# Attention and a routed MLP on one core: router rows on 128 partitions, gathered rows scaled by ScalarE and added by TensorE, late statistics moved, dummy products in the head, and a new order

## The chip, the core and the metric

The kernel runs on one NeuronCore of a Trainium2 chip. The core has five engines with instruction queues of their own: TensorE (PE, with PEld for its weight loads), VectorE (DVE), ScalarE (ACT), GpSimd (POOL) and SyncE (SP, here a queue of DMAs). They meet at semaphores; each runs its own queue strictly in order. The metric is the device time of one execution, in microseconds, as the median of several runs.

## The reference

Two blocks in a row on x of 2048 rows (tokens) and 448 columns, with layer norms ahead of both. The first is attention with 16 heads of 28 columns that share one key and one value head. The second scores each row with one vector, takes the best 8 rows of all 2048, and runs those 8 alone through a gated MLP of 1792 columns; the other rows pass unchanged.

```python
def _A_ref(x, wq, wk, wv, wo):
    q = (x @ wq).reshape(B, S, H, Dh).transpose(0, 2, 1, 3)
    k = x @ wk
    v = x @ wv
    p = _softmax(jnp.einsum("bhqd,bkd->bhqk", q, k) * (Dh ** -0.5), axis=-1)
    o = jnp.einsum("bhqk,bkd->bhqd", p, v)
    return o.transpose(0, 2, 1, 3).reshape(B, S, H * Dh) @ wo
def _B_ref(x, w_r, w_gate, w_up, w_down):
    r = x @ w_r
    idx = jnp.argsort(-r, axis=-1)[:, :8]
    x_sel = x[idx]
    y = (_silu(x_sel @ w_gate) * (x_sel @ w_up)) @ w_down
    y = y * _sigmoid(r[idx])
    return x + scatter(y, idx)
h = x + _A_ref(_layernorm(x), ...)
h2 = h + _B_ref(_layernorm(h), ...)
```

(shortened; the second block's residual is the normed h, so the output is h plus its norm, and for 8 rows the MLP's y on top)

## The kernel before

**Tiles.** The rows are cut into 16 blocks of 128 queries (b) and 16 tiles of 128 keys (j). A pair (b, j) has the scores of 16 heads: four strips of 128 x 512 in PSUM, made by matmuls on 32-row pieces of K (`scores`, L823). Their exponentials are made by one of two engines. On ScalarE (`act_tile`, `spill`) one ACTIVATE covers two strips, 128 x 1024, and writes P (L888). On VectorE with POOL (`dve_tile`) one TENSOR_SCALAR covers one strip and writes Y, a 16-bit integer whose bits are a rough exponential (L915); POOL adds a constant to a whole tile twice (Yc, L926), and the three versions, with values of their own weight, sum to a better one. So an ACT tile costs ScalarE two instructions and PE one group of value products; a DVE tile costs VectorE four, POOL two and PE three groups. `_ND` says how many tiles of each block go to VectorE: 87 of 256 in all. Six ACTIVATEs of block 1 run early and write into the still empty MLP weights (wg_sb, wu_sb, L874); `_EARLY` says behind how many tiles of block 0.

**Head.** `group(g)` norms a few key tiles: statistics on VectorE (bn, mv, L724), the scale on ScalarE (var, rstd), scaled rows in `of`, transposes on PE (L757) with a copy to xnT (L762), then K, V and for each block Q (`q_project`). K has two halves of partitions that hold the same keys. VectorE copies both from PSUM (L772, r = 0 and 1), or, for the groups in `_KD`, only the first, and two DMAs copy it on. POOL makes the masks tri and ident and clears K and Vs.

**Block's end.** `evict` copies the sums (Ot, L953), sends the denominators through DRAM, inverts them (Rc) and fetches them broadcast (Rb); VectorE multiplies (On, L966); `out_proj` projects, adds x, takes statistics and the router's dot product (junk, L1001), and `ln2` writes the output rows. Rows also go to `n_rows` in DRAM for a later gather.

**Tail.** `stage1` finds the best 8 of each of the first 14 blocks (best, idx), DMAs their numbers (gidx, cidx), gathers these 112 rows, and norms them again (cst, xc). `tail` finishes block 15 through PSUM alone. `last_rows` takes its statistics. A row of 112 + 256 scores on one partition (uc) is searched for its maximum 8 (top8, idx8); a product with ones sends the positions to all partitions (q16, one16), a comparison makes a one-hot matrix (oh), and products with it pick the 8 rows (xsel) and their numbers (tok). Then come gate, up and down products. The 8 output rows are read back by an indirect DMA (base, once all output rows are written), VectorE adds the MLP's yT to them (fin), and an indirect DMA writes them. `warm` runs products that nobody reads, so that PE doesn't stand idle.

**Order.** Nothing of the order on an engine is written by hand. `_Flow.plan` is a list scheduler in the kernel: each operation has a duration that the author gives, reads, writes, and a priority; the plan picks the next one for each engine, and assigns PSUM banks. The tables ahead of it (`_W`, `_LOOK`, `_WIN`, `_LATE`, `_HOLD`) steer it. So any change of a duration or a table can reorder all queues; semaphores keep the result right whatever the times. L628 is the helper that issues most matmuls, L640 that of the DMAs.

Of the kernel before, what the change touches and what calls it, by code (L numbers as in the profile page):

```python
# [25 lines left out]
class _Graph:  # L26
# [214 lines left out]
_KD = (1, 2, 4)  # L241
_EARLY = (0, 6, 9)
# [6 lines left out]
    0, 0, 0, 0, 0, 0, 0, 0, 0, 0, 0, 0, 0)  # L249
# [264 lines left out]
def _fast(nc, G, sb, ps, psb, flag, scr, rows, A_x, A_wq, A_wk, A_wv, A_wo, B_w_r, B_w_gate, B_w_up, B_w_down, out):  # L514
# [204 lines left out]
    def group(g):  # L719
# [29 lines left out]
        for a in range(t0, t1, 2):  # L749
# [9 lines left out]
            G.op(PE, [tr(k, ch) for k in range(m) for ch in range(NCH)], m * 4 * (150 if g == 0 else 80),  # L759
                 reads=[("of", a + k) for k in range(m)] + ["ident"], writes=[u.key], take=u)  # L760
# [8 lines left out]
                  for ch in range(NCH)], 4 * (145 if g == 0 else 5 + w / 2.4), reads=[("wkr", r) for r in range(4)] + ["wk_rep"] + [("xnT", t) for t in tl_],  # L769
# [47 lines left out]
    def scores(kind, b, j, k, key, tile=None, slot=(), parts=()):  # L817
# [15 lines left out]
        o = G.op(PE, [part(q, *p) for q, p in enumerate(parts)] if parts else strip, 231,  # L833
# [14 lines left out]
    def pv_op(b, key, src, v, j, reads):  # L848
# [7 lines left out]
        o = G.op(PE, [fn(i) for i in range(4)], 231, form="P", reads=reads + [("V", j), "Vone%d" % v], prio=key,  # L856
# [10 lines left out]
    def spill(end):  # L867
        while strips:
            if strips[0][0] == 1 and strips[0][1] in early:
                b, j, _, key = strips[0]  # L870
                for k, i in enumerate((0, 2)):
# [8 lines left out]
            if len(strips) < n or (end and len(strips) == 4 and n == 3):  # L880
                if not end:
# [7 lines left out]
                                                           scale=OCT), 50.0 + 426.5 * n,  # L889
# [977 lines left out]
```

## Time and profile before

| | |
|---|---|
| median of 3 runs | 348.11 us (347.79 to 348.26) |
| the profiled execution | 348.56 us, span 346.6 us |
| busy in the span | PE 318.2, ACT 325.4, DVE 319.4, POOL 190.8 us |
| ACTIVATE of scores (P) | 332, and 6 early ones |
| strips on VectorE (Y) | 348 |

A group's row has line, engine, operation, output <- input with shapes and count, then its busy time and the mean length of one in ns, then idle time of its engine just ahead of it and what ended it. A time line's row has start and length in us. The mean of an ACTIVATE is longer than its share of the time, since the next one begins before the last one's end is recorded; two starts give the pace.

### The profile page before, as it was taken

The page shows a single profiled execution, that of the slowest core. Times are in us where ns is not written, and L with a number is a line of the kernel's source. Part 1 is how long each engine was busy: PE and PEld are TensorE (multiplying, and loading weights), DVE is VectorE, ACT ScalarE, POOL GpSimd, SP SyncE. Part 2 cuts the span into 40 slices and gives each one's busy share as a digit, 9 for nine tenths or more (in the row PEclk, how much of TensorE's full clock was granted, in tenths as well). Part 3 has the DMA queues.
Part 4 walks back from the last instruction along what each step waited for, and adds up shares of the span by engine and source line. Part 5 has one row for each costly group of instructions (what it writes and reads, how often), then busy time and mean ns, then how long its engine had stood idle before and what let it go on. Part 6 is the DMA issues. An engine that isn't in the chain of part 4 may idle for free.

```text
span 346.6 us, 8725 instructions
## 1 busy us (share of the span) xinstructions
PE 318.2 (92%) x3630; PEld 105.2 (30%) x3630; DVE 319.4 (92%) x662; ACT 325.4 (94%) x387; POOL 190.8 (55%) x206
## 2 busy tenths in 40 slices
PE   3889899999999999999999998999999999999974
PEld 2644232323232322323232322323232322222334
DVE  6998997999988999999899899999999899999874
ACT  5599999999999999999999999999999999999850
POOL 8010475666545648667456566576747456775401
PEclk9999999999999999999999999999999999999995
DMA  6510000000020205020020206020101012152210
GB/s 158 138 40 3 0 3 18 20 17 18 5 85 4 84 4 168 27 60 30 8 80 5 84 4 165 4 46 16 33 4 30 7 58 85 42 152 58 60 36 9
DMA packets 18374, 16.18 MB, mean 47 GB/s; under 512 B 6574, under 2 KB 15438, under 8 KB 18330
## 3 DMA queue, kind: packets, MB, share of 16 engines
q1 hardware_dynamic: 16826, 15.01, 15.5%
q8 instruction: 29, 0.48, 0.6%
q10 hardware_dynamic: 1392, 0.45, 0.6%
q0 software_dynamic: 112, 0.12, 0.1%
q14 instruction: 15, 0.12, 0.1%
HBM read 11.78 MB, written 3.71 MB: 45 GB/s over the span
## 4 chain that ended last, share of the span: by engine, by line
ACT 83%; DVE 9%; DMA 3%; PE 3%; issue 0%; POOLq 0%; POOL 0%; ACTq 0%; DVEq 0%
ACT P L888 80%; DVE Y L915 4%; PE ps L628 2%; DMA wqx<-in_A_wq_dram 1%; ACT wg_sb L874 1%; DMA wqx<-n_rows,cidx 1%; DVE bn L724 1%; PE ps L823 1%; DMA cidx<-gidx 1%; ACT wu_sb L874 1%; DVE K L772 0%; ACT wqx L711 0%; DVE Q L806 0%; PE ps L757 0%; DVE gidx L1123 0%
## 5 line engine op out<-in xcount | busy, mean ns | idle before, releaser
L888 ACT ACTIVATE P<-ps 128x1024 bf16<-128x1024 f32 x332 | 306.8, 1287 | 0.0
L926 POOL INT64_ADD Yc<-Y x174 | 178.5, 1037 | 127.7 <-DVE Y L915 112.3
L915 DVE TENSOR_SCALAR Y<-ps 128x512 int16<-128x512 f32 x348 | 220.0, 683 | 12.0 <-PE ps L823 11.3
L823 PE MATMUL ps<-Q,K 32*128 32x512 bf16 (+1 forms) x1024 | 147.1, 386 | 14.1 <-ACT P L888 10.8
L823 PEld LDWEIGHTS ps<-Q,K 32*128 32x128 bf16 (+1 forms) x1024 | 37.7, 91 | 142.9 <-ACT P L888 122.1
L853 PE MATMUL ps<-Yc,Vs 128*32 128x512 bf16 x696 | 63.9, 385 | 0.0
L853 PE MATMUL ps<-P,Vs 128*32 128x512 bf16 x664 | 59.4, 387 | 0.0
L853 PE MATMUL ps<-Y,Vs 128*32 128x512 bf16 x348 | 34.2, 384 | 0.2 <-DVE Ot L953 0.2
L853 PEld LDWEIGHTS ps<-P,Vs 128*32 128x32 bf16 x664 | 14.1, 93 | 28.3 <-issue 26.2
L853 PEld LDWEIGHTS ps<-Yc,Vs 128*32 128x32 bf16 x696 | 15.7, 94 | 21.5 <-issue 15.8
L628 PE MATMUL ps<-xnT,wqx 112*128 112x128 bf16 x256 | 21.6, 229 | 0.0
L628 PE MATMUL ps<-wo_pad,On 128*32 128x448 bf16 (+1 forms) x244 | 18.1, 358 | 1.2 <-DVE Y L915 0.6
L628 PEld LDWEIGHTS ps<-xnT,wqx 112*128 112x128 bf16 x256 | 15.6, 102 | 7.7 <-issue 4.8
L806 DVE TENSOR_SCALAR Q<-ps,qone 128x512 bf16<-128x512 f32 (+1 forms) x16 | 11.6, 727 | 1.0 <-PE ps L628 0.9
L853 PEld LDWEIGHTS ps<-Y,Vs 128*32 128x32 bf16 x348 | 9.1, 94 | 9.3 <-issue 7.4
L966 DVE TENSOR_TENSOR On<-Ot,Rb 128x512 bf16<-128x512 f32 x15 | 11.0, 734 | 0.5 <-DMA Rb<-l_scr 0.5
L757 PE MATMUL ps<-ident,of 128*112 128x128 bf16 x64 | 6.3, 248 | 5.5 <-DVE of L737 5.5
L996 DVE TENSOR_TENSOR of<-ps,x_sb 128x448 bf16<-128x448 f32 x15 | 9.3, 619 | 1.1 <-PE ps L628 1.1
L953 DVE COPY Ot<-ps 128x512 f32<-128x512 f32 x15 | 10.3, 685 | 0.0
L724 DVE BATCH_NORM_STATS2 bn<-x_sb 128x6 f32<-128x448 bf16 x16 | 9.5, 610 | 0.0
L998 DVE BATCH_NORM_STATS2 bn<-of 128x6 f32<-128x448 bf16 x15 | 9.3, 622 | 0.1
L1001 DVE SCALAR_TENSOR_TENSOR junk<-of,w_rb 128x448 bf16<-128x448 bf16 x14 | 8.5, 611 | 0.0
(169 smaller groups left out, 141.4 us busy)
## 6 DMA issues: line engine op xcount, KB each, us to landing
Rb<-l_scr SPq DMA_DIRECT2D x15, 256.0 KB
out_dram<-of SPq DMA_DIRECT2D x16, 112.0 KB, 2.2
n_rows<-of SPq DMA_DIRECT2D x14, 113.0 KB, 2.4
x_sb<-in_A_x_dram SPq DMA_DIRECT2D x3, 448.0 KB, 4.4
wg_sb<-in_B_w_gate_dram SPq DMA_DIRECT2D x3, 448.0 KB, 6.1
wu_sb<-in_B_w_up_dram SPq DMA_DIRECT2D x3, 448.0 KB, 6.1
xnT<-in_B_w_down_dram SPq DMA_DIRECT2D x3, 448.0 KB, 7.7
wqx<-in_A_wq_dram ACTq DMA_DIRECT2D x1, 392.0 KB, 4.6
```

The source lines that it names most:

```text
L628: return lambda e: e.matmul(o() if callable(o) else o, lhsT=l, rhs=r, start=start, stop=stop)
L724: G.op(DV, lambda e, t=t: e.bn_stats(bn6[:, t, :], x_sb[:, t, :]), 516, reads=[("x", t)], writes=[("bn6", t)], after=[G.last_w[("xnT", 0)] ...
L806: G.op(DV, lambda e, c=c, src=src: e.tensor_scalar(Q[:, b % 3, c[0]:c[1], :], src(), qone[:, 0:1], None, ALU.add), 60 + n * 150, reads=[u. ...
L823: return e.matmul(ps[:, u.b[0] + q, :], lhsT=K[a:a + w, i % 2, j * 128:(j + 1) * 128], rhs=Q[a:a + w, b % 3, :, :].rearrange("p h n -> p ( ...
L853: return e.matmul(ps[32 * i:32 * i + 32, ACC, :], lhsT=Vs[:, v, j, :], rhs=src(i), start=info["first"] == o.idx, stop=info["last"] == o.idx)
L888: G.op(AC, lambda e, u=u, p=p, n=n: e.activation(P[:, p:p + n, :], ps[:, u.b[0]:u.b[0] + n, :], ACT.Exp, bias=EB, scale=OCT), 50.0 + 426.5 ...
L915: G.op(DV, lambda e, u=u, g0=g0: e.tensor_scalar(Y0[:, g0, :].bitcast(I16), ps[:, u.b[0], :], 0.0, TOP - STEP[-1], ALU.max, ALU.min), 599, ...
L926: G.op(PO, lambda e: e.int64_add(Yc[:, c, :, :].rearrange("p a b -> p (a b)").bitcast(I64), Y0[:, 4 * s:4 * s + 4, :].rearrange("p a b -> ...
L953: o = G.op(DV, lambda e: e.tensor_copy(Ot[:, rb, :], ps[:, ACC, :]), 598, reads=[pk(ACC)], writes=[("Ot", rb)], prio=b - 10.0, after=blk[b ...
L966: G.op(DV, lambda e: e.tensor_tensor(On[:, rb, :, :].rearrange("p h n -> p (h n)"), Ot[:, rb, :], Rb[:, rb, :], ALU.mult), 599, reads=[("O ...
L996: G.op(DV, lambda e: e.tensor_tensor(of[:, t, 0:D], hp(), x_sb[:, t, :], ALU.add), 535, reads=[u.key, ("x", t)], writes=[("of", t)], free=u)
L998: G.op(DV, lambda e: e.bn_stats(bn6[:, t, :], of[:, t, 0:D]), 520, reads=[("of", t)], writes=[("bn6", t)])
```

## The change

- **Tiles.** `_ND` sums to 90: three tiles go from ScalarE to VectorE and POOL. `_EARLY` puts the early ACTIVATEs behind three tiles of block 0. `_KD` is (3, 5): K of tiles 1, 2, 3, 6 and 7 gets its second half from VectorE, that of tiles 4, 5 and 8 to 11 by DMA.
- **Planner's numbers.** Durations, hops and tables are new, so all queues are ordered anew.
- **Head.** `fill` issues products of a constant tile into a bank that nobody reads: 44 at the start, 28 more between the first groups. Both halves of block 0's Q are copied by ScalarE. The masks wait for POOL's first 64-bit addition.
- **Block 14.** Its dot product with the router's vector no longer waits for its scale and is multiplied by it later; its statistics stand behind the shuffles of block 15, its scale behind their exponentials, and its output rows on ScalarE behind xc. So do those of block 15.
- **Router.** Scores are multiplied out to all 128 partitions (weights broadcast), so that maximum, positions and one-hot need no send. The 112 best are searched first and replaced by their 8 (a maximum that writes into PSUM), so the last maximum runs over 264 elements; the positions are still searched in 368.
- **Gathered rows.** xc is made by ScalarE (scale and bias) instead of VectorE.
- **End.** The base rows are added by PE (a product with the identity into the same bank), and the two halves of fin are copied by VectorE and ScalarE. The check of the denominators stands behind xsel.

```diff
-_KD = (1, 2, 4)
-_EARLY = (0, 6, 9)
+_KD = (3, 5)
+_EARLY = (3, 3, 3)
-_ND = (2, 7, 6, 3, 7, 7, 6, 5, 5, 7, 6, 5, 4, 5, 6, 6)
+_ND = (2, 6, 7, 4, 6, 6, 5, 7, 6, 6, 5, 6, 7, 5, 6, 6)
-_LOOK = 111.5
+_LOOK = 167.8
...
+    def fill(n, ns, after):
+        G.op(PE, [mm(ps[:, ACC, 0:128], idi[:, :], idi[:, :], True, True) for _ in range(n)], n * ns, reads=["idi"],
+             writes=[pk(ACC)], after=after, prio=-1999)
+
+    fill(44, 98, ())
...
     G.op(PO, lambda e: e.affine_select(ident[:, :], idi[:, :], [[-1, 128]], ALU.is_equal, 0.0, base=0, channel_multiplier=1),
-         300, reads=["idi"], writes=["ident"])
+         300, reads=["idi"], writes=["ident"], after=[lib])
...
         if g == 0:
+            fill(5, 56, [G.last_w[uk.key][0]])
             q_project(0)
+            fill(9, 56, [o for o in G.ops[-8:] if o.eng == PE][-1:])
...
-            if b == 0 and c[0] == 0:
+            if b == 0:
                 G.op(AC, lambda e, c=c, src=src: e.activation(Q[:, 0, c[0]:c[1], :], src(), ACT.Identity, bias=qone[:, 0:1]),
...
             G.op(AC, lambda e, u=u, p=p, n=n: e.activation(P[:, p:p + n, :], ps[:, u.b[0]:u.b[0] + n, :], ACT.Exp, bias=EB,
-                                                           scale=OCT), 50.0 + 426.5 * n,
+                                                           scale=OCT), 64.0 + 426.7 * n,
...
-        G.op(AC, lambda e: e.activation(st[:, t, 1:2], st[:, t, 0:1], ACT.Exp, scale=-0.5), 200, reads=[("st0", t)],
-             writes=[("st1", t)])
+        q = G.op(AC, lambda e: e.activation(st[:, t, 1:2], st[:, t, 0:1], ACT.Exp, scale=-0.5), 200, reads=[("st0", t)],
+                 writes=[("st1", t)])
+        for o in late15:
+            o.deps[q.idx] = False
+            o.deps[G.last_w["xc"][0].idx] = False
...
-        G.op(AC, lambda e: e.activation(of[:, t, 0:D], hp(), ACT.Identity, bias=st[:, t, 3:4], scale=st[:, t, 2:3]), 560,
+        o = G.op(AC, lambda e: e.activation(of[:, t, 0:D], hp(), ACT.Identity, bias=st[:, t, 3:4], scale=st[:, t, 2:3]), 560,
              reads=[u.key, ("st2", t), ("st3", t)], writes=[("of", t)], free=u)
+        o.deps[G.last_w["xc"][0].idx] = False
...
-        G.op(DV, lambda e: e.tensor_scalar(gidx[:, :], idx1[:, :], base1f[:, 0:1], None, ALU.add), 70,
-             reads=["idx1", "base1f"], writes=["gidx"])
+        G.op(DV, lambda e: e.tensor_scalar(gidx[:, :], idx1[:, :], base1f[:, 0:1], None, ALU.add), 100,
+             reads=["idx1", "base1f"], writes=["gidx"], lock=True)
...
-        G.op(DV, lambda e: e.tensor_scalar(xc, candb, cm[:, 0:1], cst[:, 4:5], ALU.subtract, ALU.mult), 400,
-             reads=["cand", "cst4"], writes=["xc", "wq_sb", "wq_pad"] + [("wqp", c) for c in range(NCH)], lock=True)
+        G.op(DV, lambda e: e.tensor_scalar(cst[:, 5:6], cm[:, 0:1], -1.0, cst[:, 4:5], ALU.mult, ALU.mult), 62,
+             reads=["cand", "cst4"], writes=["cst5"])
+        G.op(AC, lambda e: e.activation(xc, candb, ACT.Identity, bias=cst[:, 5:6], scale=cst[:, 4:5]), 560,
+             reads=["cand", "cst4", "cst5"], writes=["xc", "wq_sb", "wq_pad"] + [("wqp", c) for c in range(NCH)], prio=-60)
...
-        comb = bank(uc, slice(0, 1), slice(0, NB + 256))
-        G.op(DV, lambda e: e.max(top8[:, :], comb()), 510, reads=[uc.key], writes=["top8"], prio=-48.5)
...
-        G.op(DV, lambda e: e.tensor_copy(q16[:, :], idx8[:, :]), 62, reads=["idx8"], writes=["q16"], prio=-48.5)
-        G.op(PE, mm(bank(uo, c=slice(0, 8)), one16[:, :], q16[:, :], True, True), 100, reads=["one16", "q16"],
-             writes=[uo.key], take=uo)
+        G.op(DV, lambda e: e.max(bank(uc, c=slice(NB + 256, NB + 264))(), bank(uc, c=slice(0, NB))()), 250, reads=[uc.key],
+             writes=["uc2"])
+        G.op(DV, lambda e: e.max(top8[:, :], bank(uc, c=slice(NB, NB + 264))()), 450, reads=["uc0", "uc1", "uc2"],
+             writes=["top8"], prio=-48.5)
+        G.op(DV, lambda e: e.max_index(idx8[:, :], top8[:, :], bank(uc, c=slice(0, NB + 256))()), 570,
+             reads=[uc.key, "uc0", "uc1", "top8"], writes=["idx8"], prio=-48.5, free=uc)
...
+                fns += [mm(bank(uy[h], slice(0, 8), yc), ident[0:8, 0:8], base[:, dc], True, False),
+                        mm(bank(uy[h], slice(0, 8), yc), yT[:, c, :], ident[:, 64 * (c // 3):128], False, True)]
+        G.op(DV, lambda e: e.tensor_copy(fin[:, half[0]], ps[0:8, uy[0].b[0], 0:256]), 330, reads=[uy[0].key], writes=["fin0"],
+             free=uy[0])
+        G.op(AC, lambda e: e.activation(fin[:, half[1]], ps[0:8, uy[1].b[0], 0:192], ACT.Copy), 330, reads=[uy[1].key],
+             writes=["fin1"], free=uy[1])
```

Line numbers of the changed kernel differ by a few to twenty: P is L896, Y L923, On L974, gidx L1135, base L1277.

More of the change, by code (lines that the diff above doesn't have):

```diff
@@ L758, in tr @@
                                              of[:, a + k, ch * CK + cut(a, ch):(ch + 1) * CK + cut(a, ch)], ident[:, :])
-            G.op(PE, [tr(k, ch) for k in range(m) for ch in range(NCH)], m * 4 * (150 if g == 0 else 80),
-                 reads=[("of", a + k) for k in range(m)] + ["ident"], writes=[u.key], take=u)
+            o = G.op(PE, [tr(k, ch) for k in range(m) for ch in range(NCH)], m * 4 * (100 if g == 0 else 80),
+                     reads=[("of", a + k) for k in range(m)] + ["ident"], writes=[u.key], take=u)
+            if g == 0:
+                fill(8, 56, [o])
+            elif g == 1:
+                fill(6, 56, [o])
             dst = xnT[0:CK, :, a * 128:(a + m) * 128]
@@ L855, in fn @@
             return run
-        o = G.op(PE, [fn(i) for i in range(4)], 231, form="P", reads=reads + [("V", j), "Vone%d" % v], prio=key,
+        o = G.op(PE, [fn(i) for i in range(4)], 226, form="P", reads=reads + [("V", j), "Vone%d" % v], prio=key,
                  after=[blk[b - 1]["evict"] if b else None])
@@ L1011, in ln2 @@
         sv = of[:, sl, D:RW].bitcast(F32)
-        G.op(AC, lambda e: e.activation(st[:, sl, 0], sv[:, :, 1], ACT.Ln, bias=ebias[:, 0:1]), 300,
-             reads=[("stf", t) for t in ts] + ["ebias"], writes=[("st0", t) for t in ts])
-        G.op(AC, lambda e: e.activation(st[:, sl, 1], st[:, sl, 0], ACT.Exp, scale=-0.5), 100, reads=[("st0", t) for t in ts],
+        ln = G.op(AC, lambda e: e.activation(st[:, sl, 0], sv[:, :, 1], ACT.Ln, bias=ebias[:, 0:1]), 175,
+                  reads=[("stf", t) for t in ts] + ["ebias"], writes=[("st0", t) for t in ts])
+        G.op(AC, lambda e: e.activation(st[:, sl, 1], st[:, sl, 0], ACT.Exp, scale=-0.5), 87, reads=[("st0", t) for t in ts],
              writes=[("st1", t) for t in ts])
@@ L1229, in tail @@
                      reads=[(nm, c) for c in range(4)] + [nm + "0", "xsel"], writes=[uh[k].key], take=uh[k])
-        G.op(AC, lambda e: e.activation(sig[:, 0:8], ps[:, ut.b[0], 8:16], ACT.Exp, scale=-1.0), 200, reads=[ut.key],
+        G.op(AC, lambda e: e.activation(sig[:, 0:8], top8[:, :], ACT.Exp, scale=-1.0), 200, reads=["top8"],
              writes=["sig0"], prio=-49)
@@ L1252, in tail @@
              130, reads=[ud[1].key, "y0"], writes=["yT"], free=ud[1])
[L1253 removed]
+        G.op(DV, lambda e: e.tensor_copy(tokf[:, :], ps[0:8, ut.b[0], 0:2]), 62, reads=[ut.key], writes=["tokf"], free=ut, prio=-49)
         G.op(DV, lambda e: e.scalar_tensor_tensor(tok[:, 0:1], tokf[:, 0:1], 128.0, tokf[:, 1:2], ALU.mult, ALU.add), 62,
```

141 lines of the change are left out of this document (70 added, 71 removed).

## Prediction

> **What bounds the kernel now.** I read the page's busy shares and its chain first, then the busy time by stretches, then the chain in order of time, then the groups and the waits, and last the time lines of the head and the tail.
>
> The first two rows are of the page, parts 1 and 4; the next three are busy times by stretch (length, then PE, PEld, DVE, ACT, POOL, the granted clock, DMA); then two pieces of the chain (start, us) and ScalarE's last activations (time line: start, us); then two groups (busy, mean ns, idle before) and one wait (total, times, longest).
>
> ```profile
> PE 318.2 (92%) x3630; PEld 105.2 (30%) x3630; DVE 319.4 (92%) x662; ACT 325.4 (94%) x387; POOL 190.8 (55%) x206
> ...
> ACT 83%; DVE 9%; DMA 3%; PE 3%; issue 0%; POOLq 0%; POOL 0%; ACTq 0%; DVEq 0%
> ```
> ```profile
> 17.00:220.00 203.00, 194.04 (x2151) 61.00 (x2149) 190.58 (x358) 203.00 (x229) 114.46 (x112) 1.00 0.14 40
> 220.00:260.00 40.00, 38.40 (x446) 11.03 (x446) 39.32 (x73) 40.00 (x44) 24.62 (x24) 1.00 0.09 22
> 260.00:327.00 67.00, 63.33 (x711) 17.25 (x703) 63.23 (x128) 66.94 (x77) 41.05 (x40) 1.00 0.23 63
> ```
> ```profile
> 16.89 1.94 ACT wg_sb L874 x2
> ...
> 39.66 87.16 ACT P L888 x95
> ```
> ```profile
> 314.72 12.21 ACT L888 ACTIVATE P<-ps 128x1024 bf16<-128x1024 f32 x13
> ```
> ```profile
> L888 ACT ACTIVATE P<-ps 128x1024 bf16<-128x1024 f32 x332 | 306.8, 1287 | 0.0
> L915 DVE TENSOR_SCALAR Y<-ps 128x512 int16<-128x512 f32 x348 | 220.0, 683 | 12.0 <-PE ps L823 11.3
> ```
> ```profile
> DVE Y L915 <- PE ps L823: 11.3, 35, 0.8
> ```
>
> From 16.89 to 326.93 us ScalarE is never free: it is the bound there, at 87.16/95 = 0.9175 us an activation. VectorE is close behind: 190.58 + 39.32 + 63.23 = 293.1 busy of 310, so 16.9 us idle, 11.3 of them waiting for scores. PE is busy for nearly as long, but its matmuls overlap, and it waits for ScalarE; I take it as no bound. So there are three parts: a head until 16.9, a stretch in which two nearly full engines share the tiles, and a tail of 19.7 us that is a chain.
>
> **Head: what is ready when the steady run begins.**
>
> ```profile
> 1.74 1.69 POOL L697 MEMSET K<- 128x1920 bf16 x1
> ```
> ```profile
> 7.21 1.86 PE L628 MATMUL ps<-xnT,wqx 112*128 112x128 bf16 x16
> 9.70 0.47 DVE L806 TENSOR_SCALAR Q<-ps,qone 128x256 bf16<-128x256 f32 x1
> ...
> 10.95 2.06 ACT L888 ACTIVATE P<-ps 128x1024 bf16<-128x1024 f32 x2
> ...
> 11.54 0.40 DVE L772 TENSOR_SCALAR K<-ps,kcol 128x128 bf16<-128x128 f32 x1
> ...
> 12.20 0.25 DVE L785 TENSOR_TENSOR Vs<-ps,vco 128x84 bf16<-128x84 f32 x1 [0.25 <-PE ps L628]
> ...
> 14.61 1.28 PE L628 MATMUL ps<-xnT,wqx 112*128 112x128 bf16 x20
> 14.91 0.53 DVE L772 TENSOR_SCALAR K<-ps,kcol 128x256 bf16<-128x256 f32 x1
> ...
> 15.69 0.72 DVE L806 TENSOR_SCALAR Q<-ps,qone 128x512 bf16<-128x512 f32 x1
> ```
>
> Before, two activations run at 10.95, and the third waits until 16.89 for Q of block 1. The order of ScalarE at this place, before:
>
> ```order
> L742 ACTIVATE of<-x_sb,nb,rstd 128x448
> L888 ACTIVATE P<-ps 128x1024 x2
> L728 ACTIVATE var<-mv,ebias 128x2
> L730 ACTIVATE rstd<-var 128x2
> L728 ACTIVATE var<-mv,ebias 128x2
> L730 ACTIVATE rstd<-var 128x2
> L874 ACTIVATE wg_sb<-ps 128x1024 x2
> ```
> and ScalarE's rows there after:
> ```order
> L896 ACTIVATE P<-ps 128x1024
> L744 ACTIVATE of<-x_sb,nb,rstd 128x448
> L896 ACTIVATE P<-ps 128x1024 x2
> L730 ACTIVATE var<-mv,ebias 128x2 x2
> L732 ACTIVATE rstd<-var 128x2 x2
> L896 ACTIVATE P<-ps 128x1024 x5
> L882 ACTIVATE wg_sb<-ps 128x1024 x2
> ```
>
> Eight activations of block 0 now stand ahead of the early ones. The first four need key tiles 0 and 1, whose second halves VectorE now makes itself, with no transfer. The fifth needs K of tiles 2 and 3, VectorE's copy that ended at 15.44. Ahead of that copy VectorE gains the second half of K of tile 1 (about 0.33) and Q of block 1 (0.65), loses half of Q of block 0 (0.38, now ScalarE's), and starts about 0.25 later, since the 1.69 us clearing of K now stands ahead of the masks on POOL. That makes 15.44 + 0.85 = 16.29, and from a copy to its activation pass 0.47 (16.42 to 16.89): 16.76. If VectorE's waits for PE on the way go (0.25 in the row of Vs, some 0.6 in all), it is 16.1. I take 16.4. By then four activations are done, not two: 2 x 0.9175 + 0.5 = 2.3 us gained.
>
> The dummies, 72 products of 128 columns, 44 of them before the first transposes, stand where PE waited anyway; I cost them at nothing. If they outlast 5.7 us they push the transposes back. The rows show PE's products in two speeds: 16 took 1.86 (0.116 each) at 7.21, 20 took 1.28 (0.064) at 14.61. Whether the dummies bring the second speed forward decides between my bounds: 16.76 keeps VectorE's waits for PE, 16.1 loses them. The Trainium skill, "TensorE: Matmul & The Clock Gate", section "What's actually happening", says that the array runs at half rate until it has been kept busy for about 3.4 us; by that rule the gate opens at an estimated 4.5 us, the head gains 2.6 and the sum below is -5.7; without it the head gains 2.0 and the sum is -5.1. The rows agree on two rates a factor of about two apart; no run here shows dummies.
>
> **The long stretch: three tiles move from ScalarE to VectorE.** The table of tiles per block sums to 87 before and 90 after. ScalarE loses 6 activations of 0.9175: 5.5 us. With 328 left after 16.4, and 1.8 us of small ones as before (310.04 - 336 x 0.9175), its last ends at 16.4 + 300.9 + 1.8 = 319.1, if it is always fed. POOL's six more additions lie in its idle time (24.62 busy of 40).
>
> VectorE gains 12 strips of 220.0/348 = 0.63: 7.6 us. What it loses:
>
> ```profile
> 29.19 1.52 DVE L772 TENSOR_SCALAR K<-ps,kcol 128x512 bf16<-128x512 f32 x2
> ```
> ```profile
> 321.32 0.49 DVE xnT L1276
> ...
> 322.01 0.32 DVE xnT L1278 x2
> ```
> ```profile
> 323.43 0.85 DVE L1123 TENSOR_SCALAR gidx<-idx,base1f 14x8 uint32<-14x8 uint32 x1
> 324.88 1.15 DVE L966 TENSOR_TENSOR On<-Ot,Rb 128x512 bf16<-128x512 f32 x1 [0.53 <-DMA Rb<-l_scr]
> ```
>
> One K copy of 512 columns (0.7) goes to transfers, the check of the sums (0.8) goes behind the router, and gidx, which POOL's last additions had stretched to 0.85, is to run free of them (0.7 less). So VectorE needs 293.1 + 7.6 - 2.2 = 298.5 of the 302.1 us from 17 to 319.1: it may idle 3.6. Its fullest window (220 to 260) idled 0.68 of 40, 1.7%; over 302 us that is 5.1, so VectorE comes 1.5 us late, and the last block with it. Between the bounds, 0 (no idle but the 3.6) and 12.9 (its present 16.9 x 302/310 = 16.5), I take the fullest window, for after the change all windows are as full.
>
> **Tail.** ScalarE's and VectorE's rows, then the DMAs:
>
> ```profile
> 330.84 0.30 ACT L1137 ACTIVATE cst<-wqx,ebias 112x1 f32<-112x1 f32 x1 [0.86 <-DMA wqx<-n_rows,cidx]
> ...
> 332.06 0.76 ACT L1030 ACTIVATE of<-of,st 128x448 bf16<-128x448 bf16 x1
> ...
> 333.05 0.20 ACT L1045 ACTIVATE st<-st 128x1 f32<-128x1 f32 x1
> ...
> 334.47 0.72 ACT L1060 ACTIVATE of<-ps,st 128x448 bf16<-128x448 f32 x1
> ```
> ```profile
> 333.87 0.54 DVE L1200 MAX8 top<-ps 1x8 f32<-1x368 f32 x1
> ...
> 335.08 0.16 DVE L1203 CAST q<-idx 1x8 f16<-1x8 uint32 x1
> ...
> 337.16 0.15 DVE L1254 SCALAR_TENSOR_TENSOR tok<-tokf 8x1 int32<-8x1 f32 x1
> ...
> 341.54 0.19 DVE L1251 TENSOR_TENSOR yT<-ps,y 128x32 bf16<-128x32 f32 x1 [0.77 <-PE ps L628]
> ...
> 342.27 0.67 DVE L1264 TENSOR_TENSOR fin<-ps,base 8x256 bf16<-8x256 f32 x2 [0.30 <-PE ps L628]
> ```
> ```profile
> 335.96 0.17 PE L628 MATMUL ps<-oh,wqx 112*128 112x8 bf16 x1 [0.50 <-DVE oh L1208]
> ```
> ```profile
> 337.82 0.89 POOL L1256 DMA_INDIRECT base<-out_dram,tok  x1 [9.32 <-DVE tok L1254]
> 343.25 0.88 POOL L1267 DMA_INDIRECT out_dram<-fin,tok  x1 [4.54 <-DVE fin L1264]
> ```
> ```profile
> DMA to landing us min/median/max: 3.8/3.8/3.8
> ```
> ```profile
> out_dram<-of SPq DMA_DIRECT2D x2, 112.0 KB, 1.7
> ```
>
> Call R the end of the last block's scale (333.25 now, 6.32 after ScalarE's last activation). VectorE's order ahead of it, before:
>
> ```order
> L915 TENSOR_SCALAR Y<-ps 128x512
> L1122 MAX_INDEX idx<-best,r 14x8
> L1123 TENSOR_SCALAR gidx<-idx,base1f 14x8
> L1126 CAST bestb<-best 14x8
> L966 TENSOR_TENSOR On<-Ot,Rb 128x512
> ```
> and VectorE's rows there after:
> ```order
> L923 TENSOR_SCALAR Y<-ps 128x512 x8
> L1132 COPY r<-ps 14x128
> L1133 MAX best<-r 14x8
> L1134 MAX_INDEX idx<-best,r 14x8
> L974 TENSOR_TENSOR On<-Ot,Rb 128x512
> L1135 TENSOR_SCALAR gidx<-idx,base1f 14x8
> L1138 CAST bestb<-best 14x8
> ```
>
> gidx now stands behind On, which waits for the transfer of Rb. That landed at 324.88, 2.05 ahead of ScalarE's end; with On (0.6) and gidx (0.1) behind it, gidx ends 1.35 ahead of the end, not 2.65 (324.28), and the gather of candidates, which waits for it on POOL, is 1.3 later; cst and the last block's scale queue behind that gather on ScalarE. Against that, block 14's two scalings (L1030's 0.76 and its twin L1026, 1.5 together) no longer stand between cst and R, as the next rows show. I take R at 6.32 + 1.3 - 1.5 = 6.1 after the end; either alone would give 4.8 or 7.6.
>
> The first maximum, over the 112 best, stands behind the two shuffles and 14 small products; bn of block 14 and the two On queue behind it on VectorE. The shuffles cover the products, and ScalarE's logarithms cover the rest: nothing, but 0.3 if they don't.
>
> Behind R: the maximum runs over 264 elements, not 368 (0.1 less); cast, product and the cast beside it go (335.08 to 335.96 becomes some 0.35): the one-hot products start at R + 2.15, 0.55 earlier. The scaling of the gathered rows on ScalarE (about 0.65) ends at about the same R + 2.1. So yT ends at R + 7.8 instead of 8.5. The last copy splits over VectorE and ScalarE (0.25 less). By these alone it loses 1.0 behind R.
>
> But look at ScalarE around R (L1045, after L1055), before:
>
> ```order
> L1137 ACTIVATE cst<-wqx,ebias 112x1
> L1139 ACTIVATE cst<-cst 112x1
> L1026 ACTIVATE xnT<-of,st 128x448
> L1030 ACTIVATE of<-of,st 128x448
> L1043 ACTIVATE st<-of,ebias 128x1
> L1045 ACTIVATE st<-st 128x1
> L1058 ACTIVATE xnT<-ps,st 128x448
> L1060 ACTIVATE of<-ps,st 128x448
> ```
> and ScalarE's rows there after:
>
> ```order
> L1036 ACTIVATE xnT<-of,st 128x448
> L1149 ACTIVATE cst<-wqx,ebias 112x1
> L1053 ACTIVATE st<-of,ebias 128x1
> L1151 ACTIVATE cst<-cst 112x1
> L1055 ACTIVATE st<-st 128x1
> L1071 ACTIVATE xnT<-ps,st 128x448
> L1251 ACTIVATE sig<-top 128x8
> L1160 ACTIVATE wqx<-wqx,cst 112x448
> L1073 ACTIVATE of<-ps,st 128x448
> L1040 ACTIVATE of<-of,st 128x448
> ```
>
> Before, the output rows of block 14 were done ahead of R and those of block 15 at R + 1.94. Now both stand last and end near R + 3.5. The read of the eight base rows waits for both writes: issue and landing 1.7 to 2.2, about 0.5 to POOL's start, 3.8 to landing: R + 9.5 to 10.1, instead of R + 8.4. PE now needs them before the last products, and idles some 2 us for them; with the products and the copies the final write starts at R + 11.1, not R + 10.0. From R on the tail is 1.1 longer, and with R's 0.2 it is 0.9.
>
> **Sum.** -2.3 - 5.5 + 1.5 + 0.9 = -5.4. The profiled execution took 348.56 (span 346.6 and 1.96 around it), so it becomes 343.2; the median shown, 348.11, lies 0.45 below it: 342.7.
>
> **Rivals.**
> - The rows land in time. If the base rows are there when yT is, and VectorE's slack suffices, the sum is -2.3 - 5.5 - 1.0 - 0.2 = -9.0: 339.1 (338.8 with the short head). For it: the tail's other steps all shorten. Against it: the DMA rows above.
> - VectorE takes over as the bound. It idled 16.9 us waiting for an order that PE had fixed, although ScalarE set the pace; if that idle stays, VectorE is up to 12.9 late: -7.8 + 0.9 + 12.9 = +6.0, 354.1. It is slower than before from 6.9 us late on, an idle of 10.5 in 302 (3.5%). For it: 35 waits up to 0.8. Against it: in 220 to 260 both engines were full at once.
> - The change cancels itself: part of that lateness, 6.2 to 7.6 us, leaves 347.4 to 348.8. The fifth group of keys, whose second half now comes by transfer, adds up to 1 us to it.
>
> **How the numbers follow.** The forecast (341 to 346) 0.55; in time 0.20; VectorE late by 5 to 6 (346 to 347.4) 0.11; cancelled 0.05; slower 0.09. A measurement here tells 0.2% (0.7 us) from nothing. Faster 0.86, same 0.05, slower 0.09. The range 338.7 to 347.2 leaves out the slower ones and the edge of the fast one.
>
> **What would show it.** Right: the steady run of ScalarE starts near 16.4 with four activations behind it; VectorE idles under 2% and ScalarE shows idle before L896; L1277 starts about 2 us after tok, and the last products wait for base. Wrong: ScalarE idles for more than 4 us, or the base rows land ahead of yT, or the fifth activation waits past 17.

## Result, and the profile after

The changed kernel takes 343.27 us in the median of four runs (342.33 to 343.59); the kernel before, run beside it, 348.02 (347.79 to 348.26). The ratio is 0.986, interval 0.984 to 0.988: faster by 1.4%, and 0.6 us from the 342.7 forecast. The profiled execution took 343.59, its span 341.3 (before 348.56 and 346.6). It is the longest of the four, whose spans are 340.1 to 341.3, so what is read from its tail below stands at the long end.

The page of the changed kernel, parts 1, 4 and 5:

```profile
PE 322.9 (95%) x3728; PEld 113.7 (33%) x3728; DVE 321.3 (94%) x673; ACT 320.6 (94%) x384; POOL 196.4 (58%) x210
...
ACT 89%; DVE 5%; PE 3%; issue 1%; DMA 1%; POOL 0%; POOLq 0%; DVEq 0%
...
L896 ACT ACTIVATE P<-ps 128x1024 bf16<-128x1024 f32 x326 | 301.1, 1175 | 1.0 <-PE ps L831 1.0
...
L923 DVE TENSOR_SCALAR Y<-ps 128x512 int16<-128x512 f32 x360 | 224.4, 683 | 5.8 <-PE ps L831 5.0
```

ScalarE's share of the chain rises from 83% to 89%; twelve more strips stand on VectorE, and its idle time ahead of them falls from 12.0 to 5.8.

ScalarE's time line where the steady run begins and where its last activations stand:

```profile
15.11 1.01 ACT L896 ACTIVATE P<-ps 128x1024 bf16<-128x1024 f32 x1
16.49 3.77 ACT L896 ACTIVATE P<-ps 128x1024 bf16<-128x1024 f32 x4 [0.38 <-PE ps L831]
...
307.02 12.25 ACT L896 ACTIVATE P<-ps 128x1024 bf16<-128x1024 f32 x13
```

Then the busy time from 17 to 319 (length, then PE, PEld, DVE, ACT, POOL, granted clock, DMA):

```profile
17.00:319.00 302.00, 294.92 (x3294) 93.66 (x3297) 294.48 (x561) 301.99 (x340) 185.25 (x181) 1.00 0.16 44
```

The fifth activation starts at 16.49, the last ends at 319.27 (before 326.93), and ScalarE is never free between: that is 7.66 us gained. The tail behind it grew from 19.67 to 22.03, so 2.36 were lost again. Here is its time line, from R (the end of the last block's scale, 325.31) on:

```profile
325.11 0.20 ACT L1055 ACTIVATE st<-st 128x1 f32<-128x1 f32 x1
...
328.17 0.99 SPq L636 DMA_DIRECT2D out_dram<-of  x2
...
328.72 0.14 DVE L1275 SCALAR_TENSOR_TENSOR tok<-tokf 8x1 int32<-8x1 f32 x1
...
331.36 0.35 PE L624 MATMUL ps<-guT,xnT 128*128 128x8 bf16 x8
...
331.86 0.69 DVE L1304 SCALAR_TENSOR_TENSOR xnT<-Ot,xnT 128x512 f32<-128x512 f32 x1
...
332.49 1.42 PE L624 MATMUL ps<-guT,xnT 128*128 128x8 bf16 x48 [0.77 <-issue]
...
333.13 0.89 POOL L1277 DMA_INDIRECT base<-out_dram,tok  x1 [10.65 <-DVE xnT L1304]
...
334.01 0.19 DVE L1272 TENSOR_TENSOR yT<-ps,y 128x32 bf16<-128x32 f32 x1 [0.56 <-PE ps L624]
...
336.04 0.26 PE L624 MATMUL ps<-base,ident 8*8 8x128 bf16 x1 [2.02 <-DMA base<-out_dram,tok]
...
337.61 0.32 ACT L1290 ACTIVATE fin<-ps 8x192 bf16<-8x192 f32 x1 [7.35 <-PE ps L624]
338.85 0.88 POOL L1292 DMA_INDIRECT out_dram<-fin,tok  x1 [4.83 <-ACT fin L1290]
```

tok is ready at 328.86, yet the gather of the base rows starts at 333.13, and the last products wait 2 us for it. The trace names VectorE's check L1304 as what released the gather. But the landing times of the two row writes, from issue (least, median, most), point at the writes:

```profile
L636 SPq DMA_DIRECT2D out_dram<-of x2: 338/345/352, 328.2 to 328.8; - x2
...
DMA to landing us min/median/max: 1.7/2.5/3.4
```

One write took 3.4 us, where both took 1.7 before. And at 329.4 one packet of instructions is fetched; the transfers of 329.4 to 329.6 (packets, MB, share of 16 engines over 0.2 us):

```profile
q8 instruction: 1, 0.02, 48.8%
q1 hardware_dynamic: 19, 0.01, 15.8%
```

That packet took 0.488 x 16 x 0.2 = 1.56 us of one DMA engine, while the row writes were under way.

### The profile page after: what moved, and what is told of

Read it like the earlier page. It is cut to its first block, busy times and chain, and to the rows that moved or that the text cites. A ratio compares the mean times of both kernels' runs of the same rounds, so it can differ in the third digit from the quotient of the medians.

```text
span 341.3 us, 8935 instructions
## 1 busy us (share of the span) xinstructions
PE 322.9 (95%) x3728; PEld 113.7 (33%) x3728; DVE 321.3 (94%) x673; ACT 320.6 (94%) x384; POOL 196.4 (58%) x210
## 4 chain that ended last, share of the span: by engine, by line
ACT 89%; DVE 5%; PE 3%; issue 1%; DMA 1%; POOL 0%; POOLq 0%; DVEq 0%
ACT P L896 86%; PE ps L624 2%; DVE bn L726 1%; ACT wg_sb L882 1%; DMA base<-out_dram,tok 1%; DVE K L778 1%; PE ps L861 1%; ACT wu_sb L882 1%; DVE xnT L768 0%; PE ps L831 0%; DVE On L1183 0%; DVE mv L728 0%; DVE Ot L1170 0%; ACT xnT L1071 0%; DVE xnT L1304 0%
## 5 line engine op out<-in xcount | busy, mean ns | idle before, releaser
L896 ACT ACTIVATE P<-ps 128x1024 bf16<-128x1024 f32 x326 | 301.1, 1175 | 1.0 <-PE ps L831 1.0
L934 POOL INT64_ADD Yc<-Y x180 | 184.7, 1038 | 116.3 <-DVE Y L923 97.5
L923 DVE TENSOR_SCALAR Y<-ps 128x512 int16<-128x512 f32 x360 | 224.4, 683 | 5.8 <-PE ps L831 5.0
L831 PE MATMUL ps<-Q,K 32*128 32x512 bf16 (+1 forms) x1024 | 152.7, 385 | 4.0 <-ACT P L896 1.8
L831 PEld LDWEIGHTS ps<-Q,K 32*128 32x128 bf16 (+1 forms) x1024 | 41.2, 91 | 126.0 <-ACT P L896 93.2
L861 PE MATMUL ps<-Yc,Vs 128*32 128x512 bf16 x720 | 66.6, 384 | 0.2
L861 PE MATMUL ps<-P,Vs 128*32 128x512 bf16 x652 | 62.5, 388 | 1.2 <-DVE Ot L961 0.9
L861 PEld LDWEIGHTS ps<-P,Vs 128*32 128x32 bf16 x652 | 15.6, 93 | 34.2 <-issue 31.2
L814 DVE TENSOR_SCALAR Q<-ps,qone 128x512 bf16<-128x512 f32 x15 | 11.2, 744 | 0.0
L974 DVE TENSOR_TENSOR On<-Ot,Rb 128x512 bf16<-128x512 f32 x15 | 10.7, 716 | 0.0
L778 DVE TENSOR_SCALAR K<-ps,kcol 128x256 bf16<-128x256 f32 (+2 forms) x12 | 6.3, 560 | 1.7 <-PE ps L624 1.7
```

What stands on the lines that cost most here:

```text
L778: G.op(DV, lambda e, r=r: e.tensor_scalar(K[:, r, sl], ps[:, uk.b[0], 0:w], kcol[:, r:r + 1], kcol[:, 2 + r:3 + r], ALU.mult, ALU.add), 19 ...
L814: G.op(DV, lambda e, c=c, src=src: e.tensor_scalar(Q[:, b % 3, c[0]:c[1], :], src(), qone[:, 0:1], None, ALU.add), 60 + n * 150, reads=[u. ...
L831: return e.matmul(ps[:, u.b[0] + q, :], lhsT=K[a:a + w, i % 2, j * 128:(j + 1) * 128], rhs=Q[a:a + w, b % 3, :, :].rearrange("p h n -> p ( ...
L861: return e.matmul(ps[32 * i:32 * i + 32, ACC, :], lhsT=Vs[:, v, j, :], rhs=src(i), start=info["first"] == o.idx, stop=info["last"] == o.idx)
L896: G.op(AC, lambda e, u=u, p=p, n=n: e.activation(P[:, p:p + n, :], ps[:, u.b[0]:u.b[0] + n, :], ACT.Exp, bias=EB, scale=OCT), 64.0 + 426.7 ...
L923: G.op(DV, lambda e, u=u, g0=g0: e.tensor_scalar(Y0[:, g0, :].bitcast(I16), ps[:, u.b[0], :], 0.0, TOP - STEP[-1], ALU.max, ALU.min), 599, ...
```

## Experiments

My theory: ScalarE sets the stretch; in the tail the row writes, met by that fetch, hold the gather; and adding the base rows on TensorE is dear. Rivals: VectorE's check holds it; VectorE sets the stretch; the dummies or the new order brought the gain. Each kernel is the changed one but for the edit shown. Each trace is of one execution, and medians were taken in several rounds, so the ratio to the kernel before, run beside each, is the safer comparison.

| kernel | median us | ratio to before, interval | span | ScalarE's last activation ends | from there to the span's end |
|---|---|---|---|---|---|
| before | 348.0 to 348.3 | | 346.6 | 326.93 | 19.7 |
| changed | 343.27 | 0.986 (0.984 to 0.988) | 341.3 | 319.27 | 22.0 |
| block 14's rows early | 341.74 | 0.982 (0.981 to 0.983) | 339.2 | 319.23 | 20.0 |
| check late | 345.23 | 0.991 (0.989 to 0.992) | 343.7 | 319.51 | 24.2 |
| TensorE kept busy | 345.78 | 0.993 (0.992 to 0.994) | 343.9 | 319.24 | 24.7 |
| 58 of 72 dummies out | 342.92 | 0.985 (0.983 to 0.987) | 340.8 | 321.14 | 19.7 |
| 93 tiles | 353.53 | 1.015 (1.013 to 1.016) | 351.6 | 322.1 | 29.5 |
| 87 tiles | 347.70 | 0.999 (0.997 to 1.001) | 345.7 | 325.09 | 20.6 |
| wide dummies | 341.89 | 0.980 (0.979 to 0.982) | 339.9 | 320.16 | 19.7 |
| rows early, VectorE adds | 341.60 | 0.981 (0.979 to 0.983) | 338.7 | 319.53 | 19.2 |
| VectorE adds | 342.03 | 0.982 (0.981 to 0.984) | 339.7 | 319.28 | 20.4 |
| all three | 341.54 | 0.981 (0.980 to 0.982) | 338.8 | 319.92 | 18.9 |

**Block 14's output rows early.**

```diff
-        for o in late15:
-            o.deps[q.idx] = False
-            o.deps[G.last_w["xc"][0].idx] = False
```

> The output rows of block 14 (L1040) are no longer held behind the scaling of the gathered rows; on ScalarE they stand ahead of L1071, where ScalarE idled 0.74 us, and nothing else moves. Theory: the gather of the base rows waited for the second of two row writes, issued 0.6 us apart and landing after 3.4 us. With one write left near R + 2.9 it lands after 1.7, the gather starts near R + 5 (not R + 7.8), its rows are there before yT, and the span falls by 2 to 2.5 us, to about 339. Rival, VectorE's check L1304, which the trace names as what the gather waited for: the gather stays at R + 7.8 and the span within 0.4 us of the changed kernel's. Second rival, a lone late write is as slow: gather at R + 6.7, 1.0 us gained.

Three rows of its tail (R is 325.27):

```profile
330.90 0.89 POOL L1277 DMA_INDIRECT base<-out_dram,tok  x1 [8.46 <-DVE gu L1263]
...
333.95 0.26 PE L624 MATMUL ps<-base,ident 8*8 8x128 bf16 x1 [0.24 <-DVE flag L1311]
...
336.76 0.89 POOL L1292 DMA_INDIRECT out_dram<-fin,tok  x1 [4.96 <-ACT fin L1290]
```

The one late write landed after 1.8, the gather started at R + 5.6, its rows were there before yT, and the span of the profiled execution fell by 2.1 (the median time by 1.5). So the late rows held the tail, as the prediction said, and L1304 did not: its end came at 333.27, behind the gather. The last products started 2.1 earlier, but the final write still came 2.8 behind them.

**The check behind yT.**

```diff
-  ... else 1005, after=late)
+  ... else 1005, after=late if n == 0 else [G.last_w["yT"][0]])
-  ... lock=True, after=[] if n == 0 else [n_])
+  ... lock=True, after=[] if n == 0 else [G.last_w["yT"][0]])
```

> VectorE's check of the last block's sums (L1302 and L1304 over 512) stands behind yT instead of ahead of it; the rest is the changed kernel. Theory, the row writes hold the gather: it stays near R + 7.8, the span within 0.4 us of the changed kernel's (the check itself is covered by the wait for the base rows). Rival, the check held it: the gather starts between R + 4 and R + 7 and the span falls by 0.8 to 2.5 us.

```profile
333.33 0.89 POOL L1277 DMA_INDIRECT base<-out_dram,tok  x1 [10.60 <-DMA out_dram<-of]
...
339.06 0.88 POOL L1292 DMA_INDIRECT out_dram<-fin,tok  x1 [4.84 <-DVE flag L1311]
```

With the check out of the way the gather stayed at R + 7.8, and the trace now names the row write (3.3 us to landing). The name of L1304 before was a coincidence: it ended at 332.55, 0.35 behind the landing of the second write, if that is the one of 3.4. The other kernels agree: in the six whose last landing is certain, the gather began 0.9 to 1.0 behind it, wherever L1304 stood, and here it is 0.9 too. My second number missed: the span grew by 2.4, not under 0.4. The final write landed after 4.0 us instead of 2.0, and the transfers of 340.2 to 340.4 show why that is plausible, three packets of instructions at once:

```profile
q8 instruction: 1, 0.02, 51.7%
q14 instruction: 2, 0.02, 28.6%
```

**TensorE kept busy while it waits.**

```diff
+        warm(9, [G.last_w["yT"][0]])
```

> Nine dummy products of 448 columns on TensorE between yT and the last eight products, in its 2.0 us of waiting for the base rows; the rest is the changed kernel. Theory: the last eight products took 1.55 us (0.19 each) because TensorE had stood idle; behind the dummies they take 0.8 or less and the span falls by about 0.7. Rival: they are slow by their shape (weights on 8 partitions, alternating with 128): still 1.5 us, no change; if the dummies outlast the base rows, up to 0.5 us slower.

TensorE's time line, then three stretches with the granted clock third from the right:

```profile
335.02 3.54 PE L624 MATMUL ps<-x_sb,ident 128*128 128x448 bf16 x9 [1.08 <-DVE flag L1311]
...
338.50 0.26 PE L624 MATMUL ps<-base,ident 8*8 8x128 bf16 x1
```
```profile
335.00:338.00 3.00, 2.98 (x9) 1.20 (x9) 0.17 (x2) 0.00 (x0) 0.00 (x0) 0.50 0.03 9
338.00:339.00 1.00, 1.00 (x5) 0.24 (x3) 0.00 (x0) 0.00 (x0) 0.00 (x0) 0.50 0.00 0
339.00:340.00 1.00, 0.88 (x6) 0.40 (x5) 0.41 (x1) 0.09 (x1) 0.00 (x0) 0.90 0.00 0
```

The theory fell. At a granted clock of 0.50 the nine dummies took 3.54, not 1.8, outlasted the rows and cost 2.6, more than the 0.5 I had allowed. The clock came back near 339.2, 4.2 us after the dummies began; the Trainium skill, "TensorE: Matmul & The Clock Gate", section "What's actually happening", gives about 3.4 us of sustained work, which agrees in kind. And idleness just ahead isn't what makes the last products slow: with 0.24 idle ahead of them (the first experiment) the eight took 1.53 as well. Once the clock was back, two products of the same size followed after 0.15 and 0.14 instead of 0.19 to 0.20, so the low clock is only part of their length. The kernel before ran its four, all with weights on 128 partitions, at the same clock of 0.50 in 0.53. That speaks for the rival, the shape, but no run changes the shape alone.

**The dummies left out** (58 of 72; the batches of 5 and 9 stay).

```diff
-    fill(44, 98, ())
...
-                fill(8, 56, [o])
+                pass
...
-                fill(6, 56, [o])
+                pass
```

> The three batches of dummy products in the head are left out; no other instruction moves. Theory, as the prediction's upper bound had it: TensorE's first transposes and Q products go back to their slow rate (0.65 and 1.86 us instead of 0.40 and 1.06), VectorE waits for them again, and the fifth activation starts at 16.8 instead of 16.5: 0.3 us slower. By the clock gate of the Trainium skill's page on TensorE, all of the head's products run at half rate and it is 0.6 slower. Rival: VectorE's own chain sets the fifth activation, no change.

The changed kernel's first transposes and Q products, and then this kernel's, with its fifth activation:

```profile
5.78 0.40 PE L759 MATMUL ps<-ident,of 128*112 128x128 bf16 x4 [0.57 <-DVE of L739]
...
7.36 1.06 PE L624 MATMUL ps<-xnT,wqx 112*128 112x128 bf16 x16
```
```profile
5.78 0.64 PE L759 MATMUL ps<-ident,of 128*112 128x128 bf16 x4 [5.78 <-DVE of L739]
...
7.99 1.91 PE L624 MATMUL ps<-xnT,wqx 112*128 112x128 bf16 x16
...
17.48 3.77 ACT L896 ACTIVATE P<-ps 128x1024 bf16<-128x1024 f32 x4 [0.38 <-PE ps L831]
```

The dummies bring the fast rate forward, and these 58 are worth 1.0 us in the head, where I had expected 0.3 to 0.6. It is not the price of all 72: the five that stay took 0.69 instead of 0.44, just ahead of the Q products. Not all of the head ran at the slow rate either: the 16 Q products at 12.58 took 1.05 again. ScalarE's end came 1.87 later: 0.6 of it is a wait for scores between 200 and 220 that the changed kernel doesn't have, and 0.3 I did not find. Yet the median did not move, for the tail was 2.4 shorter: both row writes landed after 1.7, the gather started at R + 6.1, and the gap of 0.77 in the down products was gone. Nothing had been edited there; only TensorE's program is 116 instructions shorter (58 products with their weight loads), and the fetch came at 332.2, behind the writes.

**Tiles.** Three more to VectorE (the first new line, sum 93), and three back to ScalarE (the second, sum 87); the table `_MODE`, all zeros, gets three entries more or fewer with it:

```diff
-_ND = (2, 6, 7, 4, 6, 6, 5, 7, 6, 6, 5, 6, 7, 5, 6, 6)
+_ND = (2, 6, 7, 5, 6, 6, 6, 7, 6, 6, 6, 6, 7, 5, 6, 6)
+_ND = (2, 6, 6, 4, 6, 6, 5, 6, 6, 6, 5, 6, 6, 5, 6, 6)
```

> Three more tiles for VectorE (blocks 3, 6 and 10, one each; sum 93), the order made anew by the same rules. Theory, VectorE has little left: it was busy 294.5 of the 302 us from 17 to 319; 12 more strips of 0.62 make 302, while ScalarE alone would now end at 313.8. VectorE sets the end: ScalarE's last activation ends at 320 to 326, ScalarE idles 6 to 12 us, and the time is 344 to 350. Rival, room is left (a strip back to back costs only the 0.37 by which the busy time of the group grew per added strip): ScalarE's end near 314 to 317, time 338 to 341.

> Three tiles back to ScalarE (blocks 2, 7 and 12, one each; sum 87 as in the kernel before), the order made anew. Theory, ScalarE alone sets the stretch: six activations of 0.9175 more, its end at 324.8, 5.5 us slower than the changed kernel: 348.8. Rival, the new order's density and not the tiles brought the gain: ScalarE's end less than 3 us later.

The strips' group with 93 and one wait of ScalarE; then the strips with 87, and ScalarE's last activations there:

```profile
L923 DVE TENSOR_SCALAR Y<-ps 128x512 int16<-128x512 f32 x372 | 232.0, 681 | 8.8 <-PE ps L831 8.1
```
```profile
ACT Rb L1172 <- DVE Ot L1170: 11.1, 1, 11.1
```
```profile
L923 DVE TENSOR_SCALAR Y<-ps 128x512 int16<-128x512 f32 x348 | 217.3, 681 | 11.6 <-PE ps L831 10.4
```
```profile
312.07 13.02 ACT L896 ACTIVATE P<-ps 128x1024 bf16<-128x1024 f32 x14
```

With 93 ScalarE's last activation ended at 322.1, 2.8 later with six fewer to do, and ScalarE then stood 11.1 us until VectorE's last shuffle: VectorE now ends last, and the time rose by 10, more than either theory said. But VectorE was not full. Its last shuffle began at 333.1, 12.1 later than in the changed kernel; 6.9 of that is work and 5.2 more idle time (13.8 us idle from 17 to 333.2, against 8.6 from 17 to 321). Both kernels have an order made anew by rules whose numbers were set for 90; how much of the 5.2 is that order, these runs do not tell.

With 87 ScalarE's end came 5.8 later, as six activations of 0.9175 make it (5.5). So at 90 ScalarE just sets the stretch, and the gain there is the six activations. Taken whole, the kernel with 87 is level with the one before (0.999): ScalarE ends 1.8 earlier there and the tail is 0.9 longer, so without the three tiles the rest of the change wins next to nothing. The new order alone packs the same 348 strips into 217.3 us of busy time instead of 220.0.

**Wide dummies.** 18 products of 512 columns instead of 72 of 128.

```diff
-  [mm(ps[:, ACC, 0:128], idi[:, :], idi[:, :], True, True) for _ in range(n)]
+  [mm(ps[:, ACC, 0:512], idi[:, :], idi[:, :].unsqueeze(1).broadcast_to([128, 4, 128]), True, True)
+   for _ in range((n + 2) // 4)]
```

> The dummies of the head as 18 products of 512 columns instead of 72 of 128: the same columns in 54 fewer products, so TensorE's instructions of the tail stand 108 further ahead in its program; nothing else moves. Theory, the two row writes were slow (3.4 us) because a fetch of instructions (one packet of 16 KB, at 329.4, 1.6 us of one DMA engine) fell between them: with fewer instructions it comes later by about 108 instructions (some 1.5 us), the writes land after 1.7, the gather of the base rows starts near R + 6 instead of R + 7.8, and with the head unchanged (fifth activation at 16.5) the span falls by 1.5 to 2.2 us, to 339.1 to 339.8. Rival, two writes 0.6 us apart are slow by themselves: the gather stays at R + 7.8, no change.

The row writes, the gather, the down products, and the fetch (transfers of 330.8 to 331.0):

```profile
L636 SPq DMA_DIRECT2D out_dram<-of x2: 338/345/352, 329.1 to 329.7; - x2
...
DMA to landing us min/median/max: 1.7/1.7/1.7
```
```profile
332.12 1.64 PE L624 MATMUL ps<-guT,xnT 128*128 128x8 bf16 x56
...
332.34 0.89 POOL L1277 DMA_INDIRECT base<-out_dram,tok  x1 [8.97 <-DVE gu L1263]
```
```profile
q8 instruction: 1, 0.02, 30.2%
```

The tail's program and data are the changed kernel's, and only the fetch moved (1.7 us behind the first write's issue, not 1.2, and 0.97 us long). The two writes, as close together as before, now landed after 1.7 each; the gather started at R + 6.1 and yT came at R + 7.85, as predicted for the change; the median fell by 1.4. The tail is 2.3 shorter; ScalarE's last activation came 0.9 later, of which 0.3 lies in the head, where kernels with an unedited head differ as much. So two close writes are not slow by themselves, and the fetch soon behind them is what made one late; the last section has the other kernels, which agree. The gap in the down products went too. It stood behind the eighth product (0.21 to 0.77) in every kernel whose TensorE program is unchanged up to there, and in none of the three in which it is 108 or 116 instructions shorter. That ties it to a place in the program; that it is a wait for the next block of instructions was not shown.

**VectorE adds the base rows.** Alone, and with the early rows:

```diff
-                fns += [mm(... ident[0:8, 0:8], base[:, dc], True, False),
-                        mm(... yT[:, c, :], ..., False, True)]
+                fns += [mm(... yT[:, c, :], ..., True, True)]
-        G.op(DV, ... tensor_copy(fin[:, half[0]], ps...) ...)
-        G.op(AC, ... activation(fin[:, half[1]], ps..., ACT.Copy) ...)
+        G.op(DV, ... tensor_tensor(fin[:, half[0]], ps..., base[:, half[0]], ALU.add) ...)
+        G.op(DV, ... tensor_tensor(fin[:, half[1]], ps..., base[:, half[1]], ALU.add) ...)
```

> Only the base rows' addition goes back to VectorE (two additions into the last copies, four products on TensorE instead of eight, ScalarE's copy gone); the row writes stay late. Theory: in the changed kernel 2.85 us pass from the landing of the base rows (336.0) to the final write's start (338.85); with the four products done before the rows land, VectorE's two additions (0.67 before the change) and POOL's start (0.3) are left: 1.0 to 1.2, the final write starts near 337.1 and the span falls by 1.6 to 1.8, to 339.6. Rival: the time is POOL's own, between a semaphore and its indirect transfer: under 0.7 gained.

> The early output rows of block 14 as in the first experiment, and the base rows added by VectorE in the two last copies, as before the change, instead of by four products of TensorE. Theory: from the last products' start to the final write's start the first experiment took 2.8 us; with four products instead of eight (0.5 instead of 1.5) and one engine to wait for instead of two it takes 1.5 (as before the change, 341.79 to 343.25): the span falls by another 1.0 to 1.3, to about 338. Rival: VectorE's two additions on eight partitions (0.7) give back what the products save: no change against the first experiment, 339.2.

Alone, and then with the early rows:

```profile
335.91 0.41 DVE L1288 TENSOR_TENSOR fin<-ps,base 8x256 bf16<-8x256 f32 x1 [1.69 <-DMA base<-out_dram,tok]
336.25 0.33 DVE L1290 TENSOR_TENSOR fin<-ps,base 8x192 bf16<-8x192 f32 x1
336.89 0.88 POOL L1292 DMA_INDIRECT out_dram<-fin,tok  x1 [3.10 <-DVE fin L1290]
```
```profile
334.04 0.53 PE L624 MATMUL ps<-ident,yT 128*8 128x128 bf16 x4 [0.23 <-DVE flag L1311]
...
335.50 0.88 POOL L1292 DMA_INDIRECT out_dram<-fin,tok  x1 [3.54 <-DVE fin L1290]
```

Alone: 1.0 from the first addition's start to the write's, the span 1.6 less, the median 1.2 less, as the theory said. With the early rows the products-to-write time fell from 2.8 to 1.5 as expected, but of that 1.3 the span kept 0.5, 0.3 going to a later head, and the median 0.1, no difference. The write now landed after 2.5 us instead of 2.0, beside fetches at 335.4 and 335.6; and the time outside the span rose from 2.5 to 2.9 us (2.0 before the change, 2.3 in the changed kernel). What fills that time no trace shows.

**All three edits.**

> Three edits together: block 14's output rows early, the base rows added by VectorE, the dummies as 18 wide products. Theory: the tail of the two-edit kernel (19.2 us behind ScalarE's last activation) loses TensorE's gap of 0.45 in the down products as well, as it did with wide dummies alone, and the final write lands in 2.0 again: tail 18.2, span 337.7 to 338.2, median 340.3 to 341.0. Rival: as with wide dummies alone, ScalarE loses 0.6 in the stretch, and nothing is left against the two-edit kernel's 341.6.

The rival held: the gap went, but ScalarE's end came 0.65 later than in the changed kernel and the final write landed after 2.6. At 341.54 it ties with the two-edit kernel. Both end some 0.5% below the changed kernel and 1.9% below the one before.

## Why the prediction was right, point by point

- **Head, 2.3.** The fifth activation came at 16.49 (16.4 said): 2 x 0.9175 + 0.40 = 2.2 gained. But the dummies "at nothing" was wrong: without 58 of them it comes at 17.48, beyond my upper bound of 16.76. I had counted only VectorE's waits for PE; ScalarE's copies of Q wait there as well (1.44 us without the 58, 0.74 with them).
- **Six activations, 5.5.** Right; 87 tiles put 5.8 back.
- **VectorE late, 1.5: failed, 0 measured in ScalarE's run.** ScalarE was never idle behind 16.49. VectorE needed 294.5 us, not 298.5. Each added strip did cost 0.6, but the new order packed all strips closer, which my 220.0/348 carried over from the old order. So it could idle 7.5 of the 302 (I allowed 3.6), and did. Two of the signs I had asked for did not appear: VectorE under 2% idle (it was 2.5%), and ScalarE idle before L896. What lateness there was stands at the start of the tail: the last block's shuffle (Ot) began 1.40 behind ScalarE's end, but 0.70 behind it before the change and 0.67 with 87 tiles. It waited for products with POOL's last addition, and that for VectorE's bestb, which stands with gidx behind On:

```profile
319.07 1.04 POOL L934 INT64_ADD Yc<-Y  x1 [0.85 <-DVE bestb L1138]
...
320.67 0.01 DVE L1170 LOAD_MASK_SELECT Ot<-ps  x1 [0.22 <-PE ps L861]
```

The rival "VectorE takes over" was near: with three more tiles VectorE ends last and the time is 353.5.
- **R, 6.1 behind ScalarE's end.** 6.04, but partly by luck. The shuffle came 0.7 later, and from it to R passed 4.64 instead of 5.62, as block 14's scalings were gone from there. The gather of the candidates did begin 1.6 later (gidx ended 0.4 ahead of ScalarE's end, not 1.35), but it did not hold R as I had said: its rows landed near 324.1, when ScalarE was still busy with L1036 until 324.6, and from there to R it ran without a pause.
- **Behind R: failed in size, 1.1 said, 2.6 measured, so the tail lost 2.4 and not 0.9.** The mechanism was right: output rows late, gather late, PE waiting. The steps: gather at R + 7.8, not about R + 6 (one row write of 3.4 us for the 1.7 to 2.2 I used, and 0.9 from its landing to POOL's start for the 0.5); that is 4.3 behind tok, where my sign had said about 2; its landing 2.9, not 3.8; from landing to final write 2.85, not 1.0 to 1.6 (eight products in 1.55, then the copy and 0.9 until POOL started, 0.3 before); landing of the final write 2.0, not 2.6. yT ended at R + 8.9, not R + 7.8, mostly by the gap of 0.77.
- **The sum.** -2.2 - 5.5 + 0 + 2.4 = -5.3 against -5.4 forecast: two mis-sized terms, 1.5 each, cancelled. The mechanism of the six activations and of the late rows was right; the time is right partly by luck.
- **"The rows land in time"** became true in the first experiment, but gave 341.7 and not 339.1, because the added products and POOL's later start cost what the other steps saved.

## What to carry to other kernels

Price a balance shift between two nearly full engines from both ends: run one step further each way, and see which engine stops waiting. Keep the writes that a later gather must read off the end of the chain, and let an engine that has the operand in hand anyway do the last addition. Where a long program ends in a chain of small transfers, an edit far away can move the time by 1 to 2 us through the place at which instructions are fetched, so compare such kernels by their stages and not by their medians alone.

## What the runs showed of the hardware that I had not expected

- A fetch of instructions shares the DMA engines with the data. One packet beside the row writes took 0.96 to 1.63 us of one engine. Eight of the kernels issue two row writes 0.6 us apart. Where the fetch came 0.4 to 0.6 behind the issue of the second, one or both landed after 2.8 to 4.0 us (five kernels: the changed one, the late check, the busy TensorE, VectorE's addition alone, 87 tiles). Where it came 1.1 or more behind, both landed after 1.7 (three: wide dummies, 58 dummies out, 93 tiles). Where block 14's rows were early and one write stood alone, a fetch 1.2 to 1.3 behind it left it at 1.7 to 1.8 (two kernels). The Trainium skill, "Runtime: NRT & Kernel Launch", section "Terms", has an engine's instruction memory refilled in 16 KiB blocks; the 31 packets and 0.51 MB of that queue (q8) on the profile's page agree.
- The granted clock fell to 0.50 near 328.5 and stayed there to the end of the span, although TensorE then had 168 small products of the MLP to do; before the change it fell near 338.0, also in the gate and up products. What sets it off no run here shows.
- The releaser that the trace names can be an engine that happened to end when a transfer landed: L1304 in the changed kernel, the row write itself once L1304 was moved.
